# A new order of steps, a row spread by TensorE, and eight weight tiles at other addresses

## The chip, the cores and the metric

The kernel runs on one core of a Trainium2 chip. The metric is the device time of one execution in microseconds (us). The profile calls the engines PE (TensorE, matmul), DVE (VectorE), ACT (ScalarE), POOL (GpSimd) and SP (SyncE, whose queue issues all DMAs here). PEclk is the clock that TensorE was granted, as a share of 2.4 GHz; it takes two levels, 1.0 and 0.5 (1.2 GHz).

## The reference, cut to what matters

Three layers follow each other on 3072 tokens (4 sequences of 768). All is float32.

```python
# 1: gated linear attention, 8 heads of 40, a scan over t
m_new = maximum(f[t] + m, i[t]); f_s = exp(f[t] + m - m_new); i_s = exp(i[t] - m_new)
C = f_s * C + i_s * outer(v[t], k[t]);  n = f_s * n + i_s * k[t]
y[t] = sigmoid(o_gate[t]) * (C @ q[t]) / maximum(abs(n @ q[t]), 1)
# 2: SoLU, 320 -> 1024 -> 320
h = x @ w_in;  u = h * softmax(h);  x2 = ((u - mean(u)) / sqrt(var(u) + 1e-6) * g_ln) @ w_out
# 3: SwiGLU, 320 -> 1536 -> 320
out = (silu(x2 @ w_gate) * (x2 @ w_val)) @ w_out2
```

## The kernel before, in words

Tokens are cut into 24 tiles of 128: tile j belongs to time chunk c = j // 4 (six chunks) and sequence b = j % 4. Every tile passes layers 1 and 2 and leaves its result in `x2T`; layer 3 then runs over six groups of 512 tokens (g) and twelve slices of 128 hidden columns (f), 72 units (g, f) in all.

Nothing schedules the program by itself. The string `ORDER` lists steps as `name:index`, and each engine gets its instructions in that order; an engine that waits holds up everything behind it in its own queue. From unit `HEAD` = 18 on, `program` goes on by rule. The steps that this text names:

- Gates of a chunk, on 32 partitions (a row per sequence and head): `g0` running maximum, `g1` log decay, `g2` its running sum, `gs` three rows (DVE or POOL), `gc` their transpose (PE), `gx` copy and exponentials (ACT). `gd` writes the running sum to DRAM.
- Weights W of a tile, 128 x 8 x 128: `gb` loads a row of the sum into all 128 partitions (a DMA of 512 KB that reads what `gd` wrote), `gm` puts a large negative number above the diagonal (POOL), `we` takes eight exponentials (ACT).
- Layer 1 of a tile: `ld_qk`, `ld_vo` loads; `sc` q times k (PE), `pm` times W (DVE), `pv` times v (PE), `pd` and `cs` the chunk's outer products (PE, DVE; `vw` on POOL prepares them), `pi` the share of earlier chunks (PE), `r0` to `r2`, `ya`, `yb`, `yd` the division and the output gate.
- Layer 2 of a tile: `xT` transpose, `xh`, `xl` a split into a rounded part and its rest, `h` 16 matmuls of 512 columns, `hx`, `he`, `hu`, `hc`, `hv` softmax, product and norm, `uT` transpose, `uh`, `ul` split, `o` 24 matmuls of 320 columns, `x2`, `xc` transpose into `x2T`.
- Its weights: the inputs of type float64 come as 64-bit words. `w_in` is five chunks of 512 KB, `w_out` four of 640 KB. Each chunk is loaded (`w1l`, `w2l`), converted in four steps (`w1a` on ACT, `w1b`, `w1c`, `w1d` on DVE; `w2a` to `w2d`), rounded (`w1h`, `w2h`, ACT) and its rest taken (`w1o` on DVE or POOL, `w2o` on DVE).
- Layer 3: `gv` 16 matmuls that read weight tile `w{f}` as the stationary operand, `o2` 12 matmuls that read it as the moving one.
- `wu`: eight transposes of the identity into a PSUM bank that nobody reads.

PSUM is split into two tiles of two banks (`bank2`: `sc`, `h`, `uT`, `gv`) and four of one bank (`bank1`: the rest). A step that needs one waits until the last reader of its former content is done.

SBUF addresses follow from the tile sizes: `w0` to `w3` lie in one pool, `w4` to `w11` in another that is filled behind the five tiles `ob` and takes over the memory of layer 2's tiles.

Of the kernel before, what the change touches and what calls it, by code (L numbers as in the profile page):

```python
# [33 lines left out]
ya:0 wu:13 yb:0 w1a:3 sc:3 pm:2 gm:3 gb:4 w2h:2 ld_qk:4 ib w1b:3 we:3 ld_vo:2 yd:0:0 w1c:3 pd:0 w2l:3 w2o:2 wu:14
w1o:2 w1d:3 xT:0 w1a:4 pv:1 vw:1 xh:0 w1b:4 w1h:3 cs:0 gm:4 th:1 w1c:4 ge:1 ld_qk:5 pd:1 r0:1 w1d:4 gb:5 w1o:3 sc:4
xl:0 w1h:4 ld_vo:3 g2:2 pm:3 vw:2 th:2 pv:2 gs:2 r1:1 w1o:4:0 w2a:3 we:4 r2:1 ld_qk:6 w2b:3 h:0 r0:2 ya:1 r1:2 cs:1
gm:5 yb:1 gb:6 gn:1 pm:4 yd:1 we:5 vw:3 ld_vo:4 r2:2 ed:1 ya:2 g1:3 xT:1 ld_qx:4 hx:0 gc:2 sc:5 gx:2 w2c:3 xh:1 pd:2
yb:2 ld_qk:7 w2d:3 pv:3 xl:1 gm:6 he:0 pd:3 ld_e:4 r0:3 we:6 r1:3 pv:4 hu:0 ld_vo:5 gb:7 pm:5 ld_qx:5 zm:0 sc:6 th:3
r2:3 z0:0 w2h:3 h:1 z1:0 pm:6 qw:4 ld_e:5 th:4 hc:0 gd:2 ld_qk:8 cs:2 hv:0 ya:3 yb:3 w2o:3 uT:0 ld_qx:6 pv:5 hx:1 uh:0
gb:8 vw:4 ld_vo:6 yd:2 ul:0 he:1 ld_e:6 gm:7 pi:4 th:5 qw:5:0 o:0 we:7 r0:4 g0:4 g2:3 hu:1 ld_qx:7 hr:0 zm:1:0 z0:1  # L40
ld_qk:9 cs:3 r1:4 gm:8 r2:4 sc:7 z1:1 ya:4 hc:1 pi:5 ld_vo:7 yb:4 gb:9 pd:4 we:8 r0:5 ld_qx:8 r1:5 uT:1 pm:7 ld_e:7
pv:6 r2:5 cd:4 er:2 qw:6 uh:1 ed:2 ya:5 ld_qk:10 sc:8 cs:4 vw:5 oe:0 yd:3:0 gd:3 hv:1 yb:5 pi:6 cd:5 ul:1 xT:2 vw:6
pd:5 gs:3:0 pv:7 xh:2 gm:9 gb:10 th:6 r0:6 ld_vo:8 xl:2 r1:6 ld_e:8 pm:8 h:2 we:9 r2:6 g1:4 ya:6 ld_qk:11 yb:6 th:7
# [769 lines left out]
```

## Time and profile before

| | |
|---|---|
| median of 3 runs | 764.72 us (760.44 to 764.92) |
| profiled execution | 765.17 us, of which the span of the trace is 763.5 us |
| mean granted clock | 0.977 |
| PE, DVE, ACT, POOL busy | 738.4, 444.4, 327.1, 175.2 us |
| DMA | 62.31 MB |

The span runs from the first to the last instruction of the trace; the execution's own time is 1.7 us longer. Shares of busy time are means over layers that are limited by different things: PE is the busiest engine in all of them, and the dummy transposes count as busy.

### The profile page before, as it was taken

Reading aid. Unit: us, or ns where it says so; the run is one execution under the profiler, and the core shown is the slowest. Engines: PE = TensorE matmul, PEld = TensorE weight load, DVE = VectorE, ACT = ScalarE, POOL = GpSimd, SP = SyncE. Lnnn points to the kernel's source line nnn. Section 1 sums busy time; section 2 is a strip of 40 time slices with the busy share of each in tenths; the row PEclk is TensorE's granted clock in tenths of the full one; section 3 lists DMA queues with packets and bytes.
Section 4 is the critical chain, followed back from the end, with each engine's and each line's share of the span. In section 5 each row is a group of like instructions: output and inputs, shape, how many; then the busy total and the mean of one; then the engine's idle time right before and its main releaser. Section 6 shows DMA issues by size and latency. Waiting matters only on the chain.

```text
span 763.5 us, 11503 instructions
## 1 busy us (share of the span) xinstructions
PE 738.4 (97%) x4478; PEld 660.6 (87%) x4478; DVE 444.4 (58%) x753; ACT 327.1 (43%) x675; POOL 175.2 (23%) x237
## 2 busy tenths in 40 slices
PE   7789999999999999999998999999999999999997
PEld 7679999999999998888887889888888888888886
DVE  5795886766585688776599324333433433443433
ACT  3773655556455556665554222222232323222222
POOL 5952555544241104342352210000000000000000
PEclk9686999999999999999999999999999999999999
DMA  7974774483432233211040010000010001001000
GB/s 237 313 244 148 226 242 150 130 265 118 132 102 74 89 104 104 103 53 52 2 156 0 1 35 1 1 34 1 1 35 1 0 1 36 1 0 36 1 1 34
DMA packets 24279, 62.31 MB, mean 82 GB/s; under 512 B 3195, under 2 KB 11488, under 8 KB 24224
## 3 DMA queue, kind: packets, MB, share of 16 engines
q1 hardware_dynamic: 24224, 61.57, 24.8%
q8 instruction: 35, 0.57, 0.3%
q14 instruction: 20, 0.16, 0.1%
HBM read 57.45 MB, written 4.11 MB: 81 GB/s over the span
## 4 chain that ended last, share of the span: by engine, by line
PE 87%; DVE 6%; POOL 2%; ACT 2%; issue 2%; DMA 1%; SPq 1%; ACTq 0%; POOLq 0%
PE a L708 31%; PE c L738 15%; PE a L468 12%; PE c L531 11%; PE c L378 6%; PE a L366 3%; PE a L514 2%; PE c L392 2%; PE c L384 2%; PE c L445 2%; PE c L637 1%; DVE cc L192 1%; DMA x2T<-in_w_out_dram 1%; DVE cc L197 1%; DVE t L716 1%
## 5 line engine op out<-in xcount | busy, mean ns | idle before, releaser
L708 PE MATMUL a<-Xh,w 128*128 128x512 f32 x720 | 235.9, 393 | 3.9 <-DVE t L720 3.1
L708 PE MATMUL a<-Xl,w 128*128 128x512 f32 x432 | 168.8, 391 | 0.0
L708 PEld LDWEIGHTS a<-Xh,w 128*128 128x128 f32 x720 | 132.1, 188 | 28.7 <-ACT w L675 2.6
L716 DVE SCALAR_TENSOR_TENSOR t<-t,a 128x512 f32<-128x512 f32 x72 | 49.5, 688 | 164.7 <-ACT t L712 164.7
L738 PE MATMUL c<-w,yh 128*128 128x320 f32 x576 | 127.9, 309 | 1.1 <-ACT yh L724 1.1
L712 ACT ACTIVATE t<-a 128x512 f32<-128x512 f32 x72 | 43.0, 598 | 163.4 <-PE a L708 162.2
L738 PEld LDWEIGHTS c<-w,yh 128*128 128x128 f32 x576 | 99.1, 188 | 7.0 <-ACT yh L724 1.4
L708 PEld LDWEIGHTS a<-Xl,w 128*128 128x128 f32 x432 | 81.1, 188 | 17.9
L738 PE MATMUL c<-w,yl 128*128 128x320 f32 x288 | 89.1, 309 | 0.2 <-DVE yl L728 0.2
L724 ACT ACTIVATE yh<-t 128x512 fp32r<-128x512 f32 x72 | 45.5, 632 | 100.7 <-DVE t L720 100.7
L728 DVE TENSOR_TENSOR yl<-t,yh 128x512 fp32r<-128x512 f32 x60 | 43.2, 721 | 38.5 <-ACT yh L724 38.5
L531 PE MATMUL c<-wo_h,uh 128*128 128x320 f32 x192 | 60.5, 315 | 0.1
L351 ACT ACTIVATE W<-W,col 128x128 f32<-128x128 f32 x192 | 58.4, 392 | 4.9 <-POOL W L344 4.9
L531 PE MATMUL c<-wo_h,ul 128*128 128x320 f32 x192 | 59.6, 310 | 0.7 <-DVE ul L522 0.7
L468 PE MATMUL a<-wi_h,xh 128*128 128x512 f32 x144 | 59.2, 411 | 0.3 <-DVE P L370 0.3
L531 PE MATMUL c<-wo_l,uh 128*128 128x320 f32 x192 | 59.2, 308 | 0.0
L468 PE MATMUL a<-wi_h,xl 128*128 128x512 f32 x144 | 57.4, 398 | 0.0
L738 PEld LDWEIGHTS c<-w,yl 128*128 128x128 f32 x288 | 54.1, 188 | 0.4 <-DVE yl L728 0.4
L378 PE MATMUL c<-kvo,P 128*128 128x41 f32 x384 | 50.9, 297 | 1.7 <-issue 1.7
L378 PEld LDWEIGHTS c<-kvo,P 128*128 128x128 f32 x384 | 49.9, 210 | 2.3 <-issue 1.8
L720 DVE SCALAR_TENSOR_TENSOR t<-t,a 128x512 f32<-128x512 f32 x72 | 49.4, 687 | 2.4
L370 DVE TENSOR_TENSOR P<-a,W 128x1024 f32<-128x1024 f32 x24 | 29.1, 1214 | 24.5 <-PE a L366 16.5
(126 smaller groups left out, 1161.1 us busy)
## 6 DMA issues: line engine op xcount, KB each, us to landing
W<-gd SPq DMA_DIRECT2D x24, 512.0 KB
...
```

Of the source, the lines that this page charges most:

```text
L351: act.activation(g[:, h, :], g[:, h, :], AF.Exp, bias=cols[c][:, b * H + h:b * H + h + 1])
L370: dve.tensor_tensor(out=T["P", j], in0=T["S", j].rearrange("p (h n) -> p h n", h=H), in1=T["W", j], op=ALU.mult)
L378: pe.matmul(po[:, h * D1:(h + 1) * D1], P[:, h, :], vn[:, h, :], start=h == 0, stop=j < B and h == H - 1)
L468: pe.matmul(ph[:, fs], x, w[:, fs], start=n == 0, stop=n == 7)
L531: pe.matmul(po[:, 0:DM], x[:, fs], w[:, f, :], start=n == 0, stop=n == 3 * KF - 1)
L708: pe.matmul(p[:, s * 512:s * 512 + GT], w, x, start=n == 0, stop=n == 7)
L712: act.activation(T["t", g, f], T["gv", g, f][:, 0:GT], AF.Tanh, scale=0.5)
L716: dve.scalar_tensor_tensor(out=t, in0=t, scalar=1.0, in1=p[:, 0:GT], op0=ALU.add, op1=ALU.mult)
L720: dve.scalar_tensor_tensor(out=t, in0=t, scalar=0.5, in1=p[:, 512:512 + GT], op0=ALU.mult, op1=ALU.mult)
L724: act.activation(T["yh", g, f], T["t", g, f], AF.Copy)
L728: alu[e].tensor_tensor(out=T["yl", g, f], in0=T["t", g, f], in1=T["yh", g, f].bitcast(F32), op=ALU.subtract)
L738: pe.matmul(T["acc", g][t][:, 0:DM], x[:, ts], w, start=f == 0 and n == 0, stop=f == KF2 - 1 and n == 2)
```

## The change

It replaces the list up to unit 18 and three things beside it.

- The order: chunk 0's and chunk 1's gates, now on DVE, and the load and conversion of `w_in` (fifth chunk first) stand at the head; `w_out` comes behind them. One `wu` is left of eighteen.
- For tiles 0 and 1 the row is spread by TensorE: `gb` multiplies a column of the identity, read 128 times, with the running sum, into two PSUM banks (`bank2`). `we` takes its exponentials from there into W, and `gm` then clears the part above the diagonal. Their two DMAs are gone.
- Sizes: `halfneg`, `gcol` and `ob` are padded differently (5 x 48 x 4 = 960 bytes for `ob`), and `w4` to `w11` begin 960 bytes lower. Counted in bytes, `w0` to `w3` begin at multiples of 128 in both kernels, `w4` to `w11` 64 behind one before and at multiples of 128 now; the same holds of the four tiles of `w_in` and `w_out`.
- `w2a` uses two temporary tiles in turn instead of three.

```diff
 ORDER = """
-im w1l:0 ld_rows wu:0 ld_qk:0 w2l:0 wu:1 w1a:0 w1l:1 g0:0 w1b:0 g1:0:0 wu:2 g2:0 g0:1 gd:0 gs:0 w1c:0 ld_qk:1 wu:3
...
+g0:0 ld_rows g1:0:0 g2:0 w1l:4 ib gs:0:0 w1l:0 w1a:4 gc:0 gb:0 g0:1 g1:1:0 ld_vo:0 g2:1 w1l:2 gx:0 w1a:0 ld_qk:0 w1b:4
...
-    halfneg = w1p.tile([128, 16], F32, name="halfneg")[:, 0:1]
+    halfneg = w1p.tile([128, 32], F32, name="halfneg")[:, 0:1]
...
-    NQ = 4
+    NQ, NP = 4, 2
...
     def gb(j):
         c, b = divmod(j, B)
+        if j < NP:
+
+            T["gw", j] = bank2()
+            for h in range(H):
+                n = b * H + h
+                pe.matmul(T["gw", j][:, h * L:(h + 1) * L], ident[0:BH, n:n + 1].to_broadcast([BH, 128]), T["gl", c],
+                          start=True, stop=True)
+            return
         T["W", j] = ak.tile([128, H, L], F32, tag="W", name="W", bufs=3)
...
     def gm(j):
+
         pool.affine_select(out=T["W", j], in_=T["W", j], pattern=[[0, H], [1, L]], compare_op=ALU.is_ge,
-                           fill=NEG, base=0, channel_multiplier=-1)
+                           fill=0.0 if j < NP else NEG, base=0, channel_multiplier=-1)
 
     def we(j):
         c, b = divmod(j, B)
+        if j < NP:
+            T["W", j] = ak.tile([128, H, L], F32, tag="W", name="W", bufs=3)
         g = T["W", j]
+        x = T["gw", j].rearrange("p (h n) -> p h n", h=H) if j < NP else g
         for h in range(H):
-            act.activation(g[:, h, :], g[:, h, :], AF.Exp, bias=cols[c][:, b * H + h:b * H + h + 1])
+            act.activation(g[:, h, :], x[:, h, :], AF.Exp, bias=cols[c][:, b * H + h:b * H + h + 1])
...
-    gcol = w1p.tile([128, KF], F32, name="gcol")
+    gcol = w1p.tile([128, 24], F32, name="gcol")[:, 0:KF]
...
-        T["w2", n] = wk.tile([128, FF], F32, tag=("ul", "e", "uh", "ul")[n], name="wc", bufs=1)[:, 0:2 * DM]
+        T["w2", n] = wk.tile([128, FF], F32, tag=("ul", "uh", "ul", "uh")[n], name="wc", bufs=1)[:, 0:2 * DM]
...
-            ob = px["b"].tile([128, DM + 8], F32, tag="ob", name="ob", bufs=5)[:, 0:DM]
+            ob = px["b"].tile([128, 376], F32, tag="ob", name="ob", bufs=5)[:, 0:DM]
```

PE's instructions before, from tile 0's `pv` (L378) to tile 1's; L637 is `wu`, L366 `sc`, L392 `pd`, L445 `xT`, and c and a are PSUM tiles of one and of two banks:

```order
L378 MATMUL c<-kvo,P 128x41 x8
L637 MATMUL c<-ident 128x128 x8
L366 MATMUL a<-qk 128x128 x8
L637 MATMUL c<-ident 128x128 x8
L366 MATMUL a<-qk 128x128 x8
L392 MATMUL c<-vw,kvo 120x3x41 x2
L392 MATMUL c<-vw,kvo 120x2x41
L637 MATMUL c<-ident 128x128 x8
L445 MATMUL c<-ident,y 128x128 x3
L378 MATMUL c<-kvo,P 128x41 x8
```

The same place now, from the one `wu` on (here L648) to the first matmul of `h` (L479); lines moved, so L377 is `sc`, L389 `pv`, L403 `pd`, L456 `xT`:

```order
L648 MATMUL c<-ident 128x128 x8
L377 MATMUL a<-qk 128x128 x8
L389 MATMUL c<-kvo,P 128x41 x8
L403 MATMUL c<-vw,kvo 120x3x41 x2
L403 MATMUL c<-vw,kvo 120x2x41
L389 MATMUL c<-kvo,P 128x41 x8
L377 MATMUL a<-qk 128x128 x16
L403 MATMUL c<-vw,kvo 120x3x41 x2
L403 MATMUL c<-vw,kvo 120x2x41
L456 MATMUL c<-ident,y 128x128 x3
L389 MATMUL c<-kvo,P 128x41 x8
L479 MATMUL a<-wi_h,xh 128x512
```

Of the 15 `wu` that stood ahead of the first `h` one is left; two `gb` (not shown) stand ahead of it, and `sc` of tile 4 went behind `h`.

DVE's instructions that end in the first `ul` (L522) before; L370 is `pm`, L404 `cs`, L632 `w2o`, L472 `hx`, L498 `hc`:

```order
L370 TENSOR_TENSOR P<-a,W 128x1024
L498 TENSOR_SCALAR e<-e,z 128x1024
L404 TENSOR_TENSOR C_798<-c,bmask 120x328
L432 SCALAR_TENSOR_TENSOR th<-th,rc 128x320
L436 SCALAR_TENSOR_TENSOR y<-c,th 128x320
L632 SCALAR_TENSOR_TENSOR wo_l<-wc,gcol,wo_h 128x320 x2
L472 TENSOR_REDUCE nm<-a 128x1
L522 TENSOR_TENSOR ul<-a,uh 128x1024
```

And now (L643 `w2o`, L196 `w2d`, L264 `qw`, L418 `cs`, L436 `r1`, L533 `ul`):

```order
L643 SCALAR_TENSOR_TENSOR wo_l<-wc,gcol,wo_h 128x320 x2
L196 SCALAR_TENSOR_TENSOR wc<-x2T,wc 128x640
L432 TENSOR_SCALAR rc<-c 128x8
L264 TENSOR_TENSOR qT<-qT,E 120x384
L418 TENSOR_TENSOR dc<-c,bmask 120x328
L436 SCALAR_TENSOR_TENSOR rc<-c,rc 128x8
L643 SCALAR_TENSOR_TENSOR wo_l<-wc,gcol,wo_h 128x320 x2
L436 SCALAR_TENSOR_TENSOR rc<-c,rc 128x8
L533 TENSOR_TENSOR ul<-a,uh 128x1024
```

The last two conversions of `w_out` now stand right ahead of `ul`, where `pm`, `hc` and `hx` of the first tiles stood.

## Rows read from the trace of the kernel before

**Rows 1.** The page: busy time, the clock in 40 slices, the group `pm`.

```profile
PE 738.4 (97%) x4478; PEld 660.6 (87%) x4478; DVE 444.4 (58%) x753; ACT 327.1 (43%) x675; POOL 175.2 (23%) x237
...
PEclk9686999999999999999999999999999999999999
...
L370 DVE TENSOR_TENSOR P<-a,W 128x1024 f32<-128x1024 f32 x24 | 29.1, 1214 | 24.5 <-PE a L366 16.5
```

**Rows 2.** Windows: length, busy us of each engine, clock, DMA share, GB/s.

```profile
0.00:75.60 75.60, 62.84 (x410) 57.68 (x411) 52.89 (x100) 39.88 (x103) 44.13 (x58) 0.77 0.74 238
...
79.10:400.00 320.90, 315.34 (x2201) 286.67 (x2201) 235.91 (x438) 183.07 (x391) 117.74 (x168) 1.00 0.38 124
```

**Rows 3.** Windows of 2 us where the clock changes, columns as in Rows 2.

```profile
14.00:16.00 2.00, 2.00 (x13) 2.00 (x13) 1.99 (x2) 0.58 (x3) 1.92 (x3) 0.64 0.73 237
...
42.00:44.00 2.00, 2.00 (x17) 2.00 (x16) 1.18 (x3) 1.25 (x3) 0.16 (x1) 0.81 1.00 261
...
56.00:58.00 2.00, 1.25 (x6) 1.28 (x7) 1.85 (x4) 2.00 (x8) 0.00 (x0) 0.60 0.82 308
...
70.00:72.00 2.00, 2.00 (x10) 1.54 (x9) 1.35 (x3) 0.28 (x2) 1.55 (x3) 0.98 0.00 0
```

**Rows 4.** Timeline: start, duration, instruction, idle before it and what ended that.

```profile
3.05 0.47 DVE L277 TENSOR_TENSOR_SCAN mt<-rows,mt 32x128 f32<-32x128 f32 x1 [1.68 <-DMA rows<-in_gates_dram]
...
6.32 0.43 DVE L188 TENSOR_SCALAR wc<-wc 128x512 int32<-128x512 int32 x1 [2.79 <-ACT wc L184]
6.66 0.27 DVE L284 TENSOR_TENSOR lf<-rows,mt 32x128 f32<-32x128 f32 x1
...
8.42 0.65 DVE L192 SCALAR_TENSOR_TENSOR wc<-x2T,wc 128x512 int32<-128x512 int32 x1
...
13.10 4.84 PE L637 MATMUL c<-ident 128*128 128x128 f32 x32
...
74.38 1.23 DVE L522 TENSOR_TENSOR ul<-a,uh 128x1024 fp32r<-128x1024 f32 x1 [0.76 <-ACT uh L518]
```

**Rows 5.** The chain that ended last, in order of time: start, duration, what.

```profile
27.95 3.32 PE c L378 x16
...
33.01 2.01 PE a L366 x16
...
38.93 1.44 PE c L392 x6
...
48.40 3.81 PE a L468 x16
...
55.08 1.68 issue
...
75.64 3.56 PE c L531 x24
79.20 1.09 PE a L366 x16
80.29 0.83 PE c L384 x6
81.12 0.64 PE c L392 x6
81.76 0.87 PE a L514 x8
82.63 1.71 PE c L378 x16
...
86.26 0.33 PE c L445 x3
```

**Rows 6.** PE's timeline in group 5: first matmuls of units f = 0, 4, 11.

```profile
691.13 0.63 PE L708 MATMUL a<-Xh,w 128*128 128x512 f32 x2
...
712.77 0.63 PE L708 MATMUL a<-Xh,w 128*128 128x512 f32 x2
...
750.79 0.63 PE L708 MATMUL a<-Xh,w 128*128 128x512 f32 x2
```

More of the change, by code (lines that the diff above doesn't have):

```diff
@@ L34 @@
[L34 to L43, printed above, removed]
@@ L99 @@
-ev:0 o2:1:0 gt:1:3 yh:1:2 gw:1:3 gy:1:3 gv:1:4 yl:1:2 yh:1:3 o2:1:1 gt:1:4 gw:1:4 gy:1:4 gv:1:5 yl:1:3 yh:1:4 yl:1:4:1
-o2:1:2 gt:1:5 gw:1:5 gy:1:5 o2:1:3 yh:1:5 yl:1:5 o2:1:4
+g0:0 ld_rows g1:0:0 g2:0 w1l:4 ib gs:0:0 w1l:0 w1a:4 gc:0 gb:0 g0:1 g1:1:0 ld_vo:0 g2:1 w1l:2 gx:0 w1a:0 ld_qk:0 w1b:4
+ld_qk:1 we:0 w1a:2 gs:1:0 w1b:0 w1c:4 gb:1 g0:2 w1c:0 w1d:4 gc:1 gd:0 ld_vo:1 we:1 w1b:2 w1d:0 sc:0 w1l:1 wu:10 w1h:4
+sc:1 w1l:3 w1c:2 im gb:2 ld_qk:3 er:1 gd:1 g0:3 g1:2:0 vw:0 w1o:4:0 g2:2 w1a:1 gm:0 pm:0 gm:1 ld_qk:2 gb:3 w1h:0
@@ new lines @@
+gs:2:0 pv:0 w1d:2 ld_vo:2 w1b:1 pd:0 w1o:0:0 pm:1 w1a:3 w1b:3 w1h:2 w1c:1 ld_vo:4 r0:0 w1d:1 pv:1 r1:0 gm:2 th:0 w1c:3
+sc:2 r2:0 w2l:0 ya:0 gb:4 we:2 sc:3 vw:1 ld_qk:4 r0:1 yb:0 th:1 cs:0 pm:2 w1h:1 w1d:3 r1:1 yd:0 gm:3 pd:1 w1o:2:0 r2:1
+ld_vo:3 ya:1 gx:1 xT:0 xh:0 pv:2 xl:0 r0:2 w1o:1:0 w1h:3 we:3 w1o:3:0 cs:1 r1:2 yb:1 r2:2 th:2 gm:4 h:0 w2a:0 pm:3
+vw:2 yd:1 gb:5 w2b:0 vw:3 ya:2 pd:2 hx:0 w2c:0 sc:4 xT:1 we:4 xh:1 ld_qx:5 pv:3 pm:4 xl:1 he:0 h:1 g1:3 gc:2 hu:0 yb:2
+w2l:1 ed:1 z0:0 vw:4 gm:5 r0:3 ld_qk:5 gb:6 w2a:1 ld_qk:6 ge:1 zm:0:0 we:5 z1:0 w2b:1 w2d:0 ld_e:5 gn:1 w2c:1 ld_vo:5
@@ new lines @@
+w2h:0 sc:5 pd:3 hc:0 ld_vo:6 w2d:1 pm:5 gm:6 gx:2 pd:4 cs:3 ld_e:4 ld_qx:6 qw:5 r1:3 cs:4 th:3 w2h:1 yd:2 r2:3 uT:0
+hx:1 vw:5 hv:0 he:1 pv:5 we:6 er:2 cs:2 w2o:1 gd:2 xT:2 ld_qx:4 ya:3 gb:7 xh:2 hr:0 pi:5 hu:1 ld_e:6 pv:4 w2l:3 sc:6
+th:5 qw:4 ld_qk:7 w2o:0 w2a:3 gm:7 r0:5 yb:3 w2l:2 r1:5 th:6 xl:2 pm:6 zm:1:0 pi:4 ed:2 gb:8 we:7 pd:5 w2b:3 r2:5
+w2a:2 ld_e:7 w2c:3 sc:7 ld_vo:7 qw:6 ya:5 w2d:3 w2h:3 pm:7 ld_e:8 yd:3:0 r0:4 ld_qx:7 w2b:2 yb:5 w2c:2 pv:6 g2:3
+ld_qx:8 w2o:3 pi:6 w2d:2 cd:4 ca:4:1 r0:6 qw:7:0 th:4 vw:6 ld_qk:8 cs:5 ld_e:9 h:2 pv:7 w2h:2 r1:6 xT:3 cd:5 ld_vo:8
@@ new lines @@
+yb:7 th:9 gb:15 z0:3 g0:5 sc:12 ld_qk:13 cs:8 ld_qk:14 pv:9 we:12 ya:8 vw:11 pi:9 o:2 ld_qk:17 hu:3 xh:4 r0:9 r1:9
+yb:8 z1:3 pm:12 xl:4 x2:0 ge:3 zm:3 hc:3 ld_e:10 uT:3 xc:0 gn:3 uh:3 h:4 ld_e:11 hv:3 ca:8 x2:1 r2:9 gb:11 gm:11
+gs:4:0 ya:9 yd:5:0 qw:10:0 th:10 ul:3 oe:2 yb:9 qw:11 we:11 gb:13 ed:3 hx:4 o:3 cd:9 pd:9 ld_vo:12 xc:1 ld_vo:13 cs:9
+yd:6 he:4 xT:5 xh:5 hu:4 pv:10 gm:13 z0:4 hr:3 zm:4:0 th:11 we:13 oe:3 yd:7 sc:11 sc:13 pi:10 pm:11 gd:4 pv:11 z1:4
+r0:10 ld_qx:13 ld_e:12 xl:5 r1:10 xd:2 pi:11 xd:3:0 vw:10 hc:4 ld_qx:12 xT:6 gm:15 pd:10 g1:5 r2:10 ya:10 gb:14
@@ new lines @@
+ld_vo:16 ld_e:13 gm:14 yb:10 uT:4 er:4 r0:11 uh:4 cd:10 hv:4 x2:2 pm:13 qw:12:0 xc:2 h:5 ul:4 ca:9:1 qw:13 pv:12 cs:10
+th:12 xh:6 g2:5 gd:5 pi:12 ld_qk:15 ca:10:1 hx:5 ld_qx:16 he:5 pv:13 we:15 xl:6 r0:12 hu:5 z0:5 r1:11 r2:11 ya:11
+yb:11 z1:5 sc:14 cd:12 zm:5 vw:12 sc:15 ld_qx:14 pd:11 we:14 pi:13 hc:5 pm:15 hr:4 r1:12 o:4 ld_e:15 pm:14 ld_qx:15
+oe:4 ld_vo:14 cs:11 th:13 r0:13 uT:5 uh:5 hv:5 x2:3 r1:13 ld_qk:16 r2:12 vw:13 r2:13 cd:11 ya:12 ld_e:14 ed:4 ya:13
+h:6 yb:12 xc:3 gb:16 xT:7 xh:7 gc:4 yb:13 pd:13 hr:5 pv:14 qw:14:0 gb:17 yd:8:0 gm:16 ld_vo:15 ul:5 ld_e:16 gx:4
@@ new lines @@
+gs:5:0 xl:7 pi:14 hx:6 pd:12 he:6 er:5 gb:19 cd:13 o:5 hu:6 z0:6 ld_qk:19 z1:6 vw:15 ca:11 cs:12 sc:17 ld_qx:17 sc:16
+we:16 yd:9 oe:5 zm:6:0 ca:12 ge:4 r0:14 xT:8 cs:13 gm:17 pv:15 th:14 we:17 qw:15 th:16 r1:14 xd:5:0 pm:16 r2:14 gn:4
+cd:14 qw:16:0 pm:17 pi:15 ya:14 gm:19 h:7 r0:15 ld_vo:18 xh:8 hc:6 hx:7 uT:6 xl:8 yd:10 yb:14 ld_qk:18 vw:14 hv:6
+pv:16 x2:5 he:7 z0:7 pi:16 hu:7 z1:7 xc:5 pd:14 zm:7 ca:13 uh:6 r1:15 xd:4:0 hc:7 r0:16 hv:7 cs:14 xT:9 h:8 ld_vo:17
+ul:6 yd:13:0 r2:15 r1:16 o:6 hx:8 hr:6 gb:18 xh:9 gb:20 uT:7 th:15 cd:16 oe:6 pv:17 ld_e:18 ld_e:17 ld_qk:23 xd:6
@@ new lines @@
+hx:13 hv:12 uh:12 ca:17:1 pd:19 cs:18 hr:12 xl:14 ya:19 ca:18:1 pv:20 xd:10 he:13 ul:12 hu:13 z0:13 o:12 ld_vo:23
+zm:13 xd:11:0 z1:13 cs:19 ld_e:23 hc:13 x2:11 uT:13 h:14 pi:20 hv:13 yb:19 uh:13 xc:11 hx:14 pv:21 th:21 r0:20 oe:12
+he:14 r1:20 r2:20 ul:13 pd:23 pi:21 yd:19:0 cd:19 xT:15 sc:22 hr:13 we:23 hu:14 ca:19 ld_qx:23 qw:22 ld_vo:22 qw:23
+sc:23 xh:15 xl:15 pm:23 o:13 z0:14 r0:21 zm:14 xd:12:0 x2:10 z1:14 r1:21 r2:21 h:15 hc:14 pm:22 oe:13 xc:10 hx:15
+hv:14 uT:14 pv:22 ya:21 yb:21 pv:23 th:23 pi:22 ya:20 yb:20 he:15 uh:14 th:22 z0:15 yd:20 pi:23 ul:14 xd:13 r0:23
@@ L101 @@
+gt:0:11 yl:1:0 gw:0:11 gy:0:11 yh:0:11 yl:0:11:1 o2:0:10 gt:1:1 gw:1:1 o2:0:11 gy:1:1 gv:1:2 yh:1:1 yl:1:1:1 gt:1:2
+gw:1:2 gy:1:2 gv:1:3 ev:0 o2:1:0 gt:1:3 yh:1:2 gw:1:3 gy:1:3 gv:1:4 yl:1:2 yh:1:3 o2:1:1 gt:1:4 gw:1:4 gy:1:4 gv:1:5
+yl:1:3 yh:1:4 yl:1:4:1 o2:1:2 gt:1:5 gw:1:5 gy:1:5 o2:1:3 yh:1:5 yl:1:5 o2:1:4
 """
```

94 lines of the change are left out of this document (35 added, 59 removed).

## The prediction, made before the changed kernel ran

> **What bounds the kernel now.** I read the page first. PE is busy for 738.4 of 763.5 us and every other engine for far less [rows 1], so the time is PE's work, plus PE's waits, plus what PE loses at the lower clock. The clock stands below 1.0 only in the first slices [rows 1]. The windows then say where the waits are: up to 75.6 us PE is busy for 62.8 us at a mean clock of 0.77, and a part of that is dummy work; from 79.1 to 400 us it waits for 5.6 us in all, at clock 1.00 [rows 2]. What can be won lies in the first 80 us, and the question there is when PE has enough work of its own.
>
> The chain of waits gives the landmarks: the first `h` starts at 48.4 us, the first `o` ends at 75.64 + 3.56 = 79.2 us [rows 5]. Between them PE's longest wait is 1.7 us, up to 56.8 us [rows 5], and behind it PE ran at half clock from about 57 to 70 us [rows 3]. I compare the two programs at the end of that first `o`, because both lists have all of `w_in` and `w_out` behind them there.
>
> **The new lead-in, leg one: DVE up to the first `pm`.** The first scan can start where it does now, at 3.05 us [rows 4]. DVE's queue then holds 31 short gate instructions, 0.27 us each by the row of one [rows 4], 8.4 us; eight conversion steps of `w_in`, three of 0.43 and five of 0.65 us [rows 4], 4.5 us; the rest of the fifth chunk, two half-width instructions that I put at 0.65 us each, 1.3 us; and `pm` itself, 1.21 us [rows 1]. The sum is 15.4 us, so tile 0's `pm` ends at about 18.5 us, if nothing is late. The loads: what `w_in` and tiles 0 and 1 need is 4.5 MB in the order of issue, 19 us at the 238 GB/s that this stretch moved [rows 2]; the last chunk's conversion stands some 4 us further on in DVE's queue, so loads just keep up. `gb` on PE and eight exponentials out of PSUM end long before DVE gets to `pm`: sixteen matmul passes on 32 rows cost like `sc`, 1.1 us at full clock and 2.0 at half [rows 5], per tile. I cost them at nothing; DVE's 15 us cover them. If that cover were gone, two times 2.0 us would show.
>
> **Leg two: PE from there to the first `h`.** PE's queue holds, behind that `pm`: three `pv`, two `pd`, two `sc`, one `xT`. At half clock these are 3 x 3.32 + 2 x 1.44 + 2 x 2.01 us [rows 5], and `xT` at twice 0.33, together 17.5 us; with a tenth of a microsecond at each wait 18.3 us. At full clock it would be 9 us. I take half clock: PE has nothing to do until 6 us and little until 18, and in the old trace the same kinds of steps kept running at 0.5 up to 42 us [rows 3]. So the first `h` starts at 18.5 + 18.3 = 36.8 us, against 48.4. DVE and ACT meanwhile finish `w_in`: the rests that the second half of `h` reads come out at about 38.5 us, before PE reaches them.
>
> **Leg three: DVE from 37 us to the first `ul`.** `r0` of tile 2 stands in DVE's queue and waits for the third `pv`, so DVE is held to 37 us; behind it stand 62 more steps, and `w_out`'s whole conversion is among them. What they take follows from the window: up to the end of the old `ul` (74.38 + 1.23 = 75.6 us [rows 4]) DVE was busy for 52.9 us [rows 2]. The new list has all of that work ahead of `ul` too, and 27 steps more (twelve gate and quotient steps, three `cs`, three `w1o` that POOL did, one `pm`, one `hu` and so on), 14.9 us by their rows. That makes 67.8 us of DVE work. Up to 37 us DVE can have done some 30 of them, which leaves 37.8; instructions in a row overlap a little, so 36 to 38, and `ul` ends at 74 to 76 us. I take 75. `sc` of tile 8 then needs `uT`'s PSUM tile, which `ul` gives back: 1.1 us, and `o` 3.56 us [rows 5]. The first `o` ends at 79.7 us, half a microsecond **later** than now.
>
> The bounds of this leg: DVE without a pause from 3.05 us would give `ul` at 70.9 us, 4 us earlier; if the 14.9 us came on top of the old 75.6, because its old pauses stay, it would be 90.5 us, 15 us later. I stay near the first, since every step ahead of `ul` but the waits for `pv` and `hx` has its input early.
>
> **What PE has done by then.** By the end of its first `o` the new list has run two `sc`, two `pv`, two `pd`, three `pi`, two `xT` and one `h` more than the old: 2 x 1.09 + 2 x 1.71 + 2 x 0.64 + 3 x 0.83 + 2 x 0.33 + 3.81 = 13.8 us at full clock [rows 5]. So the lead-in is worth 13.8 - 0.5 = **13.3 us**.
>
> **Smaller terms.** Three `wu` stood behind the first `o`, where PE is busy without a gap; each is eight transposes, 0.87 us like `uT` [rows 5]. One may lie beside a wait; I take 2 us off. DVE is still late for a tile or two after `ul` (`hc` of tile 1 comes 4 us behind it), and PE's queue waits there: 2 us on, between 0 and 4. The addresses: units f = 0 to 3 take (712.77 - 691.13) / 4 = 5.41 us, units 4 to 11 (750.79 - 712.77) / 7 = 5.43 us [rows 6]. If the start at 64 bytes behind a multiple of 128 is why, 48 units times 0.02 are 1.0 us; it may be nothing. `h` and `o` read tiles that shift the same way: `h` takes 3.81 us for 16 matmuls, where `gv` of a unit needs 5.41 less half an `o`, 3.63 us; 24 times the difference is 4 us more at the most, or nothing, or a loss elsewhere. I take 1 us in all. Two loads of 512 KB less and w_out later leave the rest of the list as it was in kind: I cost it at nothing, since PE waits for only 5.6 us between 79 and 400 us [rows 2].
>
> **The sum** against the profiled execution: 763.5 - 13.3 - 2 + 2 - 1 = 749.2 us of span, 750.9 with the 1.7 us around it. That execution lay 0.45 us above the median, so **750 us** for the median.
>
> A rule that speaks against one step. Rows first: between 13.1 and 17.9 us PE ran nothing but `wu` transposes [rows 4], and within that stretch, between 14 and 16 us, its clock rose from 0.5 to 1.0 [rows 3]. So transposes count, and the old return at 42.8 us, in the middle of `wu`, may be owed to them; without them half clock lasts to `h`. The Trainium skill, TensorE: Matmul & The Clock Gate, Part 4 (PE-mode transpose), says that transposes do not engage the full clock. By that rule the old return came from `sc`, `pv` and `pd` alone, some 15 us after PE had begun to run without a pause at 28 us. This trace disagrees with the rule, and I go by the row.
>
> **The rivals.**
> *The clock returns inside the lead-in* (it is what the rule would do): PE's steady work begins at 18.5 us, and 15 us later, at 33.5, the last 3.3 us of leg two halve. At the most all of leg two runs at full clock, 9 us earlier, but then DVE's work sets `ul` at 70.9 us. Together with no lateness behind `o` this gives 743 to 748 us. Against it stands the half clock through much of the old lead-in, dummies and all.
> *A second stretch at half clock.* The old trace fell back at 56 to 57 us, just behind its wait of 1.7 us, and stayed down for 13 us [rows 3, 5]. The new list has such waits too, between `h` of tile 1 and `h` of tile 2, where PE waits for DVE's `pm`. PE's work behind the first `h` up to the end of `o` is 33 us at full clock in 37 us, so of the 6.4 us lost some 5 show: 755 us.
> *Given back later.* From 79 to 400 us DVE is busy 74% of the time [rows 2], and the loads of layer 3's weights wait for buffers that DVE frees. PE may arrive 13 us early at a turn that others set, and wait there: 760 to 765 us.
> *Slower.* Without dummies the clock stays at half beyond the first `h`, since PE's queue from there to `o` is light steps with waits for DVE. That work is 37 us at full clock (three `h`, five `sc` and `pv`, four `pd` and `pi`, three `xT`, `uT` and `o` [rows 5]); half clock up to the first `o` adds up to 31 us: 781 us. It decides from 28 us of half clock behind the first `h` on, that is if the clock is not back by about 65 us. Against it: in the old trace the clock came back at 70 us [rows 3], during the second `h`, and held through 79 to 88 us, where no `h` or `o` runs.
> *Nothing from the addresses*: 751 us, inside the forecast's own range.
>
> **How the numbers follow.** The forecast, 746 to 756 us, has 0.53; an earlier clock, 740 to 746, 0.14; a second half-clock stretch, 755 to 758, 0.15; given back, 759 to 767, 0.11; slower, above 772, 0.07. A measurement of this kernel tells about 1% from no change, that is 757.1 and 772.4 us. Faster than that: the forecast, the earlier clock and half of the second stretch, 0.75. Within it 0.17, slower 0.08. The range from 742 to 763 us leaves out some of the earliest clock, half of what is given back, and the slow case: 0.17 together.
>
> **What would show it.** The first `h` at 35 to 39 us, with the clock at 0.5 from about 10 us until some 3 to 6 us into `h`. DVE near 95% busy from 37 to 75 us, with `ul` ending at 73 to 78. The first `o` ending near 80 us, with `h` of tile 2 ahead of it. Then clock 1.00 and under 10 us of PE waits up to 400 us. Units of group 5 all at 5.41 us. It is wrong if the first `h` starts after 45 us (loads late, or `w1` steps blocking each other between DVE and POOL), if DVE pauses more than 5 us behind `h`, or if PE's waits between 80 and 420 us grow by as much as the lead-in gained.

## The result, and the profile after

The changed kernel took 751.86 us in the median of four runs (750.75 to 752.92), beside 764.34 us of the kernel before in the same comparison: ratio 0.9847, 95% interval 0.9811 to 0.9883, 12.5 us less. Forecast were 750 us, 742 to 763. In a second comparison it took 751.12 us (749.62 to 753.46, six runs), ratio 0.9835 (0.9806 to 0.9865). The profiled execution took 750.75 us, its span is 749.0 us; 749.2 had been summed. The sum came out right, but its terms did not: the lead-in's was 5 us too high, the three smaller ones together 5 us too low.

The page after, against [rows 1]:

```profile
PE 728.5 (97%) x4374; PEld 653.7 (87%) x4374; DVE 448.7 (60%) x780; ACT 325.6 (43%) x675; POOL 146.4 (20%) x210
...
PEclk9996999999999999999999999999999999999999
```

PE is busy for 9.9 us less, with 104 matmuls fewer: 17 `wu` are gone and two `gb` came. The clock row shows one dip (56 to 75 us) and none at the start. That start isn't to be believed, as PE's own timeline tells (start, duration, instruction, idle time before it; `h` of tile 0, L479):

```profile
20.50 3.63 PE L389 MATMUL c<-kvo,P 128*128 128x41 f32 x16 [0.55 <-DVE P L381]
...
38.63 0.63 PE L479 MATMUL a<-wi_h,xl 128*128 128x512 f32 x1
39.06 0.63 PE L479 MATMUL a<-wi_h,xh 128*128 128x512 f32 x1
...
41.10 0.39 PE L479 MATMUL a<-wi_l,xh 128*128 128x512 f32 x1
41.33 0.39 PE L479 MATMUL a<-wi_h,xl 128*128 128x512 f32 x1
...
60.79 1.97 PE L377 MATMUL a<-qk 40*128 40x128 f32 x16 [1.31 <-DVE e L492]
...
79.83 1.16 PE L377 MATMUL a<-qk 40*128 40x128 f32 x16
80.92 0.42 PE L542 MATMUL c<-wo_h,uh 128*128 128x320 f32 x1
```

The same matmul follows its forerunner by 0.43 us at 39 us and by 0.23 us at 41 us. So PE ran at half clock from its start to some 40.3 us, 2.7 us into `h`. The first entry of the clock record in this trace is that rise, at 40.5 us, and the windows print 1.00 ahead of it. Durations say what the clock was; the record says it only behind its first entry.

The trace of the second comparison (c0 below) is of the same program, and its record begins earlier. There the clock rose at 18.1 us, right behind the one `wu`, fell at 21.5 us, behind a wait of 1.45 us for the first `pm`, and was back at 42.0 us:

```profile
22.00:24.00 2.00, 2.00 (x10) 2.00 (x11) 1.94 (x6) 0.00 (x0) 0.00 (x1) 0.50 1.05 255
...
42.00:44.00 2.00, 2.00 (x12) 1.67 (x11) 1.09 (x3) 0.00 (x0) 1.21 (x2) 1.00 0.56 211
```

Its first `h` started at 38.08 us in place of 37.63. So the half clock of this stretch is on record there, but its course is not the same in every execution.

The second dip is in the record (windows, columns as in [rows 2]):

```profile
0.00:75.60 75.60, 66.92 (x398) 61.62 (x399) 66.40 (x139) 42.25 (x114) 33.95 (x47) 0.91 0.74 241
...
60.00:62.00 2.00, 1.21 (x12) 1.21 (x14) 2.00 (x6) 1.49 (x3) 0.00 (x0) 0.74 0.66 214
62.00:64.00 2.00, 2.00 (x14) 1.78 (x13) 1.80 (x4) 1.83 (x6) 0.00 (x0) 0.50 0.85 283
74.00:76.00 2.00, 2.00 (x9) 1.64 (x8) 2.00 (x6) 1.93 (x3) 2.00 (x2) 0.85 0.14 35
...
84.55:749.00 664.45, 652.60 (x3907) 583.72 (x3905) 374.84 (x629) 280.20 (x552) 109.93 (x162) 1.00 0.18 61
```

DVE was busy for 66.4 us up to 75.6 us, where it had been busy for 52.9 [rows 2]. Its timeline shows the first `ul` and what came late ahead of it:

```profile
15.96 1.22 DVE L284 TENSOR_TENSOR lf<-lf,mt 32x128 f32<-32x128 f32 x1
...
37.87 0.17 DVE L432 TENSOR_SCALAR rc<-c 128x8 f32<-128x8 f32 x1 [2.19 <-PE c L389]
...
56.29 2.09 DVE L643 SCALAR_TENSOR_TENSOR wo_l<-wc,gcol,wo_h 128x320 fp32r<-128x320 f32 x2
58.31 1.28 DVE L443 SCALAR_TENSOR_TENSOR th<-th,rc 128x320 f32<-128x320 f32 x1
...
76.81 1.22 DVE L533 TENSOR_TENSOR ul<-a,uh 128x1024 fp32r<-128x1024 f32 x1
```

`w2o` took 2.09 us for a pair that took 0.97 elsewhere in this trace, `ya` 1.28 in place of 0.49, the gate instruction 1.22 in place of 0.28. In each case POOL was at work beside it: `gm` and `qw`, which POOL began at 56.69 and 58.01 us, and the `gm` of 15.95 us. That POOL is the cause is what c3 tests.

Where the time went, then. Up to the end of the first `o` (79.2 us before [rows 5], 84.55 now) 13.84 us of PE work more were done in 5.35 us more: the lead-in won 8.5 us (the last matmul of `o` is recorded up to 84.70 us, so this cut may be off by 0.15 us). Behind it the span was 763.5 - 79.2 = 684.3 us and is 664.45 now, 19.85 less, of which 13.84 are the work already done: 6.0 us were won there, where I had forecast 1.

### The profile page after: what moved, and what is told of

Read it like the earlier page. It is cut to its first block, busy times and chain, and to the rows that moved or that the text cites. A ratio compares the mean times of both kernels' runs of the same rounds, so it can differ in the third digit from the quotient of the medians.

```text
span 749.0 us, 11253 instructions
## 1 busy us (share of the span) xinstructions
PE 728.5 (97%) x4374; PEld 653.7 (87%) x4374; DVE 448.7 (60%) x780; ACT 325.6 (43%) x675; POOL 146.4 (20%) x210
## 4 chain that ended last, share of the span: by engine, by line
PE 83%; DVE 10%; ACT 4%; issue 2%; DMA 1%; SPq 0%; POOL 0%; DVEq 0%; ACTq 0%
PE a L719 33%; PE c L749 15%; PE a L479 11%; PE c L542 8%; PE c L389 6%; PE a L377 3%; PE a L525 3%; PE c L395 2%; PE c L403 2%; PE c L456 1%; DVE e L492 1%; DVE cc L191 1%; DVE e L509 1%; ACT e L488 1%; DMA E<-ed 1%
## 5 line engine op out<-in xcount | busy, mean ns | idle before, releaser
L479 PE MATMUL a<-wi_h,xh 128*128 128x512 f32 x144 | 59.3, 412 | 0.0
L479 PE MATMUL a<-wi_h,xl 128*128 128x512 f32 x144 | 57.1, 397 | 0.0
L362 ACT ACTIVATE W<-W,col 128x128 f32<-128x128 f32 x176 | 53.4, 391 | 0.2 <-POOL W L352 0.2
L389 PEld LDWEIGHTS c<-kvo,P 128*128 128x128 f32 x384 | 51.5, 215 | 1.7 <-DVE P L381 0.8
L389 PE MATMUL c<-kvo,P 128*128 128x41 f32 x384 | 52.2, 302 | 0.7 <-DVE P L381 0.5
L483 DVE TENSOR_REDUCE nm<-a 128x1 f32<-128x1024 f32 x24 | 29.3, 1219 | 25.3 <-PE a L479 25.3
```

Of the source, the lines that this page charges most:

```text
L362: act.activation(g[:, h, :], x[:, h, :], AF.Exp, bias=cols[c][:, b * H + h:b * H + h + 1])
L389: pe.matmul(po[:, h * D1:(h + 1) * D1], P[:, h, :], vn[:, h, :], start=h == 0, stop=j < B and h == H - 1)
L479: pe.matmul(ph[:, fs], x, w[:, fs], start=n == 0, stop=n == 7)
L483: dve.tensor_reduce(out=T["nm", j], in_=T["h", j], axis=AX.X, op=ALU.max, negate=True)
```

## The experiments

Runs of one kernel scatter by some 7 us: 17 runs of the kernel before lay between 758.5 and 765.6 us, six of the changed one between 749.6 and 753.5. So a term of 1 to 3 us is read from PE's work in one stretch of the traces, and medians decide larger ones.

**What was won behind the first `o`: sizes.** The old padding of `ob` alone (a1), that of `halfneg` and `gcol` alone (a2), and the new three in the kernel before (b1).

```diff
 a1, changed kernel
-            ob = px["b"].tile([128, 376], F32, tag="ob", name="ob", bufs=5)[:, 0:DM]
+            ob = px["b"].tile([128, DM + 8], F32, tag="ob", name="ob", bufs=5)[:, 0:DM]
 a2, changed kernel
-    halfneg = w1p.tile([128, 32], F32, name="halfneg")[:, 0:1]
+    halfneg = w1p.tile([128, 16], F32, name="halfneg")[:, 0:1]
-    gcol = w1p.tile([128, 24], F32, name="gcol")[:, 0:KF]
+    gcol = w1p.tile([128, KF], F32, name="gcol")
```

Expected of a1:

> The changed kernel with the old padding of ob alone, so that w4 to w11 stand 64 bytes behind a multiple of 128 again. Theory (the addresses of layer 3's tiles count): units f = 4 to 11 go from 5.41 back to 5.43 us, 48 x 0.02 = 1.0 us slower, 751.9 to 753 us. Rival (addresses count for nothing; units became shorter by the order of the list): no difference, within 0.3 us of the changed kernel.

Expected of a2:

> The changed kernel with the old paddings of halfneg and gcol alone, so that the tiles of w_in and w_out stand 64 bytes behind a multiple of 128 again. Theory: h takes 3.81 us again where it now takes 3.74, and o may gain as little; 22 tiles behind the first o times 0.07 are 1.5 us, so 752 to 754 us. Rival: h became shorter because fewer transfers or writes of other engines meet it; then h stays at 3.74 us and the time within 0.3 us of the changed kernel.

Expected of b1:

> The kernel before with the three new paddings and nothing else. Theory: h, and units f = 4 to 11 become shorter as in the changed kernel, 24 x 0.07 + 48 x 0.02 = 2.6 us faster, ratio 0.9966. Rival: nothing, ratio 1.000.

Measured: a1 753.09 us (751.16 to 758.86, ratio to before 0.9875, 0.9845 to 0.9904); a2 753.92 us (752.17 to 756.49; 0.9877, 0.9854 to 0.9901); b1 758.70 us (757.22 to 760.02; 0.9941, 0.9921 to 0.9962). The direction fits each time, though the intervals of a1 and a2 overlap that of the changed kernel, and b1's 5.2 us are twice its forecast; its interval just leaves out 0.9966. The size is read from the rows. First units f = 0, 4 and 11 of group 5, in the changed kernel:

```profile
677.06 0.63 PE L719 MATMUL a<-Xh,w 128*128 128x512 f32 x2
...
698.69 0.63 PE L719 MATMUL a<-Xh,w 128*128 128x512 f32 x2
...
736.53 0.63 PE L719 MATMUL a<-Xh,w 128*128 128x512 f32 x2
```

and in a1:

```profile
678.13 0.63 PE L719 MATMUL a<-Xh,w 128*128 128x512 f32 x2
...
699.77 0.40 PE L719 MATMUL a<-Xh,w 128*128 128x512 f32 x1
...
737.79 0.63 PE L719 MATMUL a<-Xh,w 128*128 128x512 f32 x2
```

Units 4 to 11 take 37.84 / 7 = 5.41 us in the one and 38.02 / 7 = 5.43 us in the other, units 0 to 3 5.41 in both. The same edit on `w_in`'s tiles, by the chain of waits of the changed kernel and of a2:

```profile
201.16 3.66 PE a L479 x16
208.66 3.66 PE a L479 x16
```

```profile
201.70 3.73 PE a L479 x16
209.28 3.73 PE a L479 x16
```

`h` is 0.07 us longer with the old address and nothing else changed, so its order and its neighbours aren't the cause. The rival, no effect, has fallen in both places. Behind the first `o` PE's work is 1.1 us more in a1 than in the changed kernel, as forecast, and 3.4 more in a2, of which `h` is 1.5. For the rest a2's trace has a stretch at half clock that the changed kernel's lacks, from 265.4 to 268.8 us:

```profile
266.00:268.00 2.00, 2.00 (x12) 2.00 (x11) 1.16 (x5) 0.00 (x0) 0.00 (x0) 0.50 0.78 273
```

At half clock 3.4 us hold 1.7 us of work, so by this estimate 0.2 us stay open. PE had not paused ahead of that fall (busy for 8.00 of 8.00 us from 256 to 264); it had run `uT`, two `pv` and part of two `pi`.

**The late `wu`** (b2: the kernel before without `wu:15` to `wu:17`). Expected:

> The kernel before without the three wu that stand behind the first o. Theory: PE is busy without a gap there, so all of 3 x 0.87 = 2.6 us goes, ratio 0.9966. Rivals: one of them lies beside a wait, 1.7 us (ratio 0.998); or the clock falls without them and the time grows.

Measured: 762.5 us (758.27 to 765.49, twelve runs), ratio 0.9987 (0.9962 to 1.0012): by itself that tells neither 1.7 nor 2.6 from nothing. PE's work behind the first `o` does; windows from there to the end, of the kernel before, of b1 and of b2:

```profile
79.20:763.50 684.30, 671.97 (x4046) 599.55 (x4045) 387.96 (x646) 283.61 (x561) 128.24 (x176) 1.00 0.20 64
```

```profile
74.40:755.80 681.40, 669.05 (x4046) 599.05 (x4045) 388.06 (x648) 283.72 (x561) 128.87 (x176) 1.00 0.20 64
```

```profile
73.98:756.60 682.62, 669.32 (x4022) 596.94 (x4021) 390.53 (x648) 283.68 (x561) 128.90 (x176) 1.00 0.20 64
```

The sizes take 671.97 - 669.05 = 2.92 us off PE's work there, the three `wu` 671.97 - 669.32 = 2.65. Together 5.57; the changed kernel has 671.97 - 652.60 - 13.84 = 5.53 less. PE's idle time there went from 12.33 to 11.85 us. That is all of the 6.0 us.

The first `o` ended at 74 us in b1 and b2, at 79.2 in the profiled run before, though nothing was changed ahead of it but addresses, in b2 nothing at all. In b2 the clock fell at 43 us and was back at 54 (windows of b2), in the run before it fell at 56 and was back at 70 [rows 3]. So the old lead-in has two courses, and its runs scatter by them: of the 17 runs of the kernel before, three show a mean clock of 0.983 or more and took 758.5 to 760.9 us, the others 0.975 to 0.980 and 761.8 to 765.6 us. Three of b1's six runs show 0.983 or more, so part of its 5.2 us is the course. Against b2's traced course the new lead-in wins only 13.84 - (84.55 - 73.98) = 3.3 us; the 8.5 hold for the course of the run before, which is the common one.

**What bounds the way to the first `ul`.** c1 fills the two pauses ahead of the second fall of the clock, c3 takes POOL's work away, c0 is the yardstick.

```diff
 c1
+    def ku(n):
+        p = T["kp", n]
+        for i in range((8, 12)[n]):
+            pe.transpose(p[:, 384:512], ident, ident)
 ...
-... gx:2 pd:4 cs:3 ... pv:4 w2l:3 sc:6
+... gx:2 pd:4 ku:0 cs:3 ... pv:4 ku:1 w2l:3 sc:6
 c3: gm:3 to gm:8, qw:4 to qw:6, cd:4, cd:5, ca:4 taken out of the list
```

Expected of c0:

> The changed kernel itself, as the yardstick of the next three: the first four runs of it gave 750.75 to 752.92 us, so a median of 751 to 753 us.

Expected of c1:

> The changed kernel with twenty dummy transposes more, in free columns of PSUM tiles that are held anyway: eight behind pd of tile 4, where PE waits 0.67 us for DVE, twelve behind pv of tile 4, where it waits 1.31 us. Theory: these two pauses let the clock fall at 61 us; filled, it stays at 1.0 from 40 us on, PE reaches sc of tile 8 seven us earlier, and waits there for the first ul, which DVE ends at 78 us whatever the clock. The first o then ends at 78.0 + 1.1 + 3.6 = 82.7 us in place of 84.55: 1.9 us faster, 749.5 to 750.5 us. Rival 1 (PE alone counts): 13.8 us at half clock become 6.9, 745 us. Rival 2: the clock falls whatever stands in the pauses, and the time stays at 752 us.

Expected of c3:

> The changed kernel without gm of tiles 3 to 8, qw of tiles 4 to 6, cd of tiles 4 and 5 and ca of tile 4: POOL's work from 29 to 78 us without what it copies and multiplies for vw. Left out are the mask above the diagonal and factors of the carried state of these tiles. Theory: from 37 to 78 us DVE's instructions took 7.4 us more than the shortest of their kind, because POOL worked beside them; without it the first ul ends 5 to 7 us earlier, at 71 to 73 us, the first o ends at 78 to 81 us, and the time is 746 to 749 us. Rival: DVE's long instructions have another cause (PSUM, ACT), they stay as long, and the time is 751 to 752 us.

Measured: c0 751.12 us; c1 753.17 us (749.72 to 753.99); c3 747.40 us (743.69 to 751.80). c1 first, its windows and its first `ul`:

```profile
60.00:62.00 2.00, 1.18 (x11) 1.06 (x11) 2.00 (x5) 1.95 (x6) 0.00 (x0) 1.00 0.07 21
62.00:64.00 2.00, 2.00 (x25) 1.71 (x24) 1.42 (x6) 1.58 (x5) 0.00 (x0) 1.00 0.85 241
68.00:70.00 2.00, 1.02 (x9) 0.87 (x8) 2.00 (x3) 0.48 (x2) 2.00 (x2) 0.97 0.82 242
70.00:72.00 2.00, 1.32 (x3) 1.13 (x4) 2.00 (x4) 0.54 (x2) 2.00 (x4) 0.50 0.40 128
```

```profile
77.76 1.23 DVE L537 TENSOR_TENSOR ul<-a,uh 128x1024 fp32r<-128x1024 f32 x1
```

A pause of 0.8 us was left at 60 us. The clock fell at 69.9 us in place of 60.9, and the first `o` came no earlier: PE waited for DVE instead (at 68 to 72 us it is busy for 2.34 of 4 us, DVE for 4.00), `ul` ended at 79.0 us. So keeping the clock up over 61 us bought nothing. Rival 1 has fallen; rival 2 has the right time, but not the clock, which did stay up over the filled pauses. Even my 1.9 us did not show, since the clock fell at the later wait. What a lead-in without any second fall would take, c1 doesn't show.

c3, DVE's first `ul` and the window from 37 us on, c3 and then the changed kernel:

```profile
72.00 1.23 DVE L533 TENSOR_TENSOR ul<-a,uh 128x1024 fp32r<-128x1024 f32 x1
```

```profile
37.00:72.00 35.00, 34.85 (x252) 31.34 (x251) 32.83 (x69) 25.32 (x68) 10.03 (x14) 0.95 0.77 237
```

```profile
37.00:72.00 35.00, 33.02 (x223) 30.06 (x223) 33.44 (x59) 23.01 (x63) 19.27 (x22) 0.84 0.73 223
```

In the same 35 us DVE does 69 instruction records in 32.8 us of work in place of 59 in 33.4. Summed over the records from 37 us to the end of `ul`, its time above the shortest of each kind is about 2 us in c3 and about 7 us in the changed kernel, and `ul` is 4.8 us earlier. So POOL beside DVE costs leg three some 5 us, and the rival has fallen. By the same count the old kernel's DVE rows up to its first `ul` hold about 7 us as well. (The traced execution of c3 was its fastest; in the medians c3 is 3.7 us ahead of c0.) What lasts longer has all its operands in SBUF; `pm`, with one input in PSUM, takes 1.17 to 1.23 us in both. The Trainium skill, GPSIMD Engine Reference, section 1 (Specifications), says the same as a rule: GpSimd shares its SBUF interface with VectorE and contends with DVE instructions that have two SBUF inputs or run in a two-port mode. The traces agree, with some 7 against 2 us.

**Leg two at full clock.** c2 and d1 move PE's dummies to the front.

```diff
 c2
+wu:0 wu:1 wu:2 wu:3 wu:4
 ...
-gs:2:0 pv:0
+gs:2:0 wu:5 wu:6 wu:7 wu:8 wu:9 wu:10 wu:11 wu:12 wu:13 pv:0
 d1
+wu:0 wu:1 wu:2 wu:3 wu:4
 ... two wu each behind gb:0, gb:1 and sc:0
-gs:2:0 pv:0
+gs:2:0 wu:11 pv:0
```

Expected of c2:

> The changed kernel with thirteen wu more: five at the very start of PE's queue, nine ahead of the first pv (one of them was there). Theory: the first five raise the clock before 7 us and the nine hold it, so that pv, pd, sc and xT up to the first h run at full clock, 9 us in place of 17; DVE paused for 0.90 + 1.15 + 2.19 = 4.2 us there, which is all that it can gain, so the first h starts at 33 to 34 us and the time is 748 us. Rival 1: the light steps let the clock fall again before the first h, 37 us as now: 752 us. Rival 2: nothing behind the first h is bound by leg two, since DVE has the same work: the first h comes at 33 us, the time stays at 751 to 752 us. A further rival is the rule of the Trainium skill, TensorE: Matmul & The Clock Gate, Part 4, that transposes do not engage the full clock: then the first pv would run at half clock from its first matmul, as now.

Expected of d1:

> The changed kernel with twelve wu in the place of its one: five at the start of PE's queue, two behind each of the two gb, two between the first two sc, one ahead of the first pv, so that PE never pauses up to 20 us and the first pv is not held back (with nine in a row it started 5.9 us behind its product). Theory: the clock stands at 1.0 from about 6 us on and through leg two, the first h starts at 33 to 34 us in place of 37.6, because DVE's 4.2 us of pauses there go, the first ul ends at 74 us, and 3 to 4 us are won: 747.5 to 748.5 us. Rival 1: the light steps let the clock fall again ahead of the first h: 751 to 752 us. Rival 2: the first ul comes earlier, but PE falls to half clock behind the first h again and loses part of it: 749 to 750 us.

Measured: c2 751.71 us (748.25 to 754.08); d1 748.85 us (747.11 to 752.99), ratio to before 0.9814 (0.9786 to 0.9842). In c2 the nine `wu` kept PE until 25.9 us, so the first `pv` came 5.9 us behind its product; the first `h` still started at 34.85 us in place of 37.63, the first `ul` ended at 76.1, and no time was won in the median. That `pv` ran at full clock (1.88 us), and the clock held up to 60 us, so rival 1 and the rival by the rule have fallen; the time is rival 2's, but not for its reason. In the trace the first `o` ended at 82.9 us, 1.65 ahead of the changed kernel's, and a stretch at half clock from 261 to 268 us, again without a pause of PE ahead of it, took that back: PE's work behind `o` is 655.46 us in place of 652.60. d1's PE (timeline, then windows):

```profile
1.42 7.51 PE L649 MATMUL c<-ident 128*128 128x128 f32 x40 [1.42 <-POOL ident masks.py:199]
...
26.19 0.39 PE L390 MATMUL c<-kvo,P 128*128 128x41 f32 x2 [1.87 <-issue]
```

```profile
24.00:26.00 2.00, 0.33 (x4) 0.17 (x2) 2.00 (x4) 1.01 (x2) 0.00 (x0) 1.00 0.77 287
26.00:28.00 2.00, 1.81 (x16) 1.84 (x16) 2.00 (x7) 2.00 (x8) 0.00 (x0) 0.98 1.05 410
28.00:30.00 2.00, 2.00 (x18) 1.92 (x19) 1.90 (x6) 1.94 (x8) 0.27 (x2) 0.50 0.99 396
```

Forty transposes in 7.51 us are 0.19 us each, where half clock takes 1.97 / 8 = 0.25 and full clock 0.87 / 8 = 0.11: within this stretch, in which PE ran nothing else, the clock rose (the record's first entry is this rise, at 7.4 us). It fell again at 28 us, behind a pause at 24 to 26 us in which PE waited for the second `pm`, which DVE ended at 26.09 us; rival 1 holds from there. The first `h` came at 37.1 us, the first `ul` ended 1 us earlier (77.0), the first `o` 1.85. So the time came near the theory's, but not by its path. d1's median is 2.3 us under that of c0; the intervals of the two ratios overlap, so d1 is the best version here only by its median.

d4 joins d1 and c1, with all twenty dummies in the tile of `pd:4`.

Expected of d4:

> The changed kernel with the twelve wu at the front and the twenty dummy transposes in PE's two waits between the first and the third h. Theory: the front gives 3 to 4 us by DVE's pauses; with DVE earlier PE's stretch at half clock behind 61 us would be the bound, and the filled waits take it away, so 746.5 to 748 us, 4 us or more below the changed kernel and faster than both kernels. Rival: the clock falls at a later wait for DVE all the same, 748 to 750 us.

Measured: 756.51 us (754.45 to 757.76), slower than either part. The cause is my edit:

```profile
61.69 3.64 PE L390 MATMUL c<-kvo,P 128*128 128x41 f32 x16 [4.15 <-DVE y L450]
```

`pd:4`'s bank is held up to the second dummies, so `pv` of tile 4 had to take a bank that DVE's `yb` gave back 4 us later; the clock fell only at the end of that wait. The question it was built for stays open.

**The row by TensorE, and the old dummies.** d2 loads W of tiles 0 and 1 by DMA again (`NP` 0, `gb:0 gb:1 gm:0 gm:1` behind `gd:0`, `we:0 we:1` behind `er:1`). d3 is the kernel before without any `wu`.

Expected of d2:

> The changed kernel with W of tiles 0 and 1 loaded by DMA as before, in the new order (mask ahead of the exponentials again). Theory: the running sum is written to DRAM at 7.7 us; a W load took 4.8 us from its issue (14.4 to 19.2 us for tile 2), and this stretch moves 290 GB/s with its DMA engines busy 80 to 100%, so two more loads of 512 KB push the rest of w_in and the tiles' inputs 3 to 4 us back: W of tile 0 is ready at 18 to 20 us, pm at 20 to 22, the first h at 40 to 41 us, and the time is 754 to 755 us. Rival: DVE's queue sets pm and the loads have 4 us to spare: 751 to 752 us.

Expected of d3:

> The kernel before without any of its eighteen wu. By my reading they brought the clock back at 42.8 us; theory: without them half clock lasts into the first h, which starts 1 to 3 us earlier in time (five wu of 1.9 us stand between 31 and 42 us) or later by up to 2 us, while three late wu save 1.5 to 2.6 us: 758 to 764 us. Rival: without them the clock is at half up to the second h, 10 us more at half clock: 768 us or more. The rule of the Trainium skill, TensorE: Matmul & The Clock Gate, Part 4, that transposes do not engage the full clock, would leave the clock's return where it is and save all of the wu that lie on PE's path, 9 us: 755 us.

Measured: d2 754.46 us (751.50 to 756.02), 3 us above c0: first `pm` at 21.1 us instead of 19.25, first `h` at 39.5, the end of the first `ul` at 79.6 us. The first `o` of its trace ended at 85.3 us, 0.75 later than in the changed kernel; that was d2's fastest execution of four, and the intervals of the two ratios overlap (0.9843 to 0.9907, 0.9806 to 0.9865). So spreading the row by TensorE is worth 1 to 3 us. The cause is not the theory's: the DMA engines were not full, as SP's queue (d2) and the windows (d2, then the changed kernel) show.

```profile
7.71 0.39 SPq L295 DMA_DIRECT2D gd<-gl  x1
13.54 0.83 SPq L348 DMA_DIRECT2D W<-gd  x2
```

```profile
12.00:14.00 2.00, 1.95 (x15) 1.78 (x14) 1.96 (x6) 1.56 (x3) 0.00 (x0) 1.00 0.11 37
```

```profile
12.00:14.00 2.00, 2.00 (x11) 1.60 (x10) 1.56 (x4) 1.38 (x6) 1.09 (x1) 1.00 1.02 273
```

The load of W reads what `gd` wrote, so it stood at the head of the queue for 5.4 us, and the last two loads of `w_in` and the rest stood behind it: they were issued at 14.89 us in place of 9.12. The changed kernel's queue stands still ahead of its first load of W too, from 10.7 to 14.4 us, but has issued all of `w_in` by then.

d3 759.16 us (757.52 to 760.74), ratio 0.9943 (0.9921 to 0.9964): the dummies cost more than they gave. Its first `h` started at 49.45 us at half clock, full clock came 2.5 us into it, and it did not fall again up to the end of the first `o` at 73.3 us (PE was busy for 18.60 of the 18.80 us from 54.4 us on). The late three are 2.65 us of the 4.7; my theory's range held, its rival did not. By the rule that the expectation names it would have been 755 us, with the clock back at 42.8 us as before; it came back at 52 us. But without dummies PE also paused on its way there, for 1.00 and 1.97 us ahead of 38.5 us, so this run alone speaks neither for nor against the rule.

## Why the prediction was right, step by step

**Leg one** (first `pm` at 18.5 us): 20.4. A gate instruction beside POOL's `gm` took 0.9 us more than its kind, two `w1b` beside POOL's `vw` and `gm` 0.85 us each in place of 0.39, and DVE waited 0.44 us for ACT; the rest was a little shorter than summed. `gb` took 3.6 us per tile at half clock, not 2.0 (2.04 at full clock, in d1), and did not cost nothing. The chain that ended last runs through it:

```profile
6.55 3.72 PE a L344 x16
10.36 2.17 ACT W L362 x8
12.53 0.56 ACT wc L183
```

ACT's `w1a` stood behind `we`, which waited for `gb`, and DVE's 0.44 us were the wait for that `w1a`.

**Leg two** (18.3 us, first `h` at 36.8): 17.1 us, 37.63. Right, half clock included: it lasted 2.7 us into `h` (3.9 in c0).

**Leg three** (`ul` at 75, bounds 70.9 and 90.5): 78.0. The bound was the right one, DVE:

```profile
0.00:78.03 78.03, 69.35 (x414) 63.75 (x414) 68.81 (x142) 42.60 (x114) 34.71 (x47) 0.91 0.74 239
37.00:78.03 41.03, 39.05 (x249) 35.14 (x249) 39.44 (x71) 24.94 (x66) 23.13 (x24) 0.83 0.66 201
```

This is the first term that was mis-sized, by 3 us. I left 37.8 us of work for it behind 37 us and no pause; DVE had 39.44 us of work and 1.6 us of pauses, the first of them up to 37.87 us for the third `pv`. All of DVE's work came to 68.8 us where 67.8 had been summed, so the rows were near enough: they come from a kernel whose POOL was busy beside DVE too, and have POOL's price in them. c3 shows how large that price is, not that the sum lacked it.

**The first `o`** (79.7): 84.55. `o` did not follow `ul` by 1.1 us, but `sc` of tile 8, which PE reached only at 79.83 us, since it had run at half clock from 61 to 74.6 us. That was my rival of a second stretch. It did happen, where it was placed, but by these rows it was worth 79.83 - 78.03 = 1.8 us and not 5: DVE would have held PE up to 78 us anyway. That is an estimate; c1, where the fall only came later, won nothing. So the lead-in won 8.5 us, not 13.3.

**Smaller terms** (-2, +2, -1): measured -2.65, -0.5 and -2.92. DVE's lateness was mis-sized most, by 2.5 us: PE's waits behind the first `o` did not grow at all. The addresses follow with 1.9: `gv` gave the 1.0 that I took, and `h` another 1.5 that I left at "4 or nothing".

The errors are 4.8 us of the lead-in that were not won and 5.0 us behind it that had not been forecast. So 750 us was right by luck, since they cancel. The range did not need that luck: either error alone would have stayed within 742 to 763 us. "Given back later" did not happen: PE's waits behind the first `o` fell by 0.5 us. The slower rival, half clock up to `o` without dummies, did not either: in the new order the clock came back 2.7 us into the first `h`, and in the old order without dummies (d3) 2.5 us into it.

The rule that I weighed, TensorE: Matmul & The Clock Gate, Part 4, of the Trainium skill, stays contradicted for these float32 transposes of the identity: d1's first forty, 7.51 us of nothing else, raised the clock by themselves. The other half of my reading holds in the first trace: `sc`, `pv` and `pd` ran for 17 us without a pause of 0.1 us ahead of `h` and stayed at half clock.
